# Scores over 128 rows for three of four batches, and value blocks 144 and 160 bytes apart, in a hashed attention with a gated feed-forward

## The chip, the core and the metric

The kernel runs on one core of a Trainium2 chip. The metric is the device time of one execution in microseconds (us); the median of three runs stands for a kernel. A core has TensorE (PE in the profile; its weight loads are PEld), VectorE (DVE), ScalarE (ACT), GpSimd (POOL) and SyncE (SP), and 16 DMA engines that all its queues share. SP issues most DMAs here, on queue q1; POOL issues the loads of the feed-forward weights, on queue q0.

## What is computed

```python
# q, k, v: (4, 8, 768, 64) f32; proj: (64, 6) f32
q_bits = (einsum('bhsd,dk->bhsk', q, proj) > 0)
k_bits = (einsum('bhsd,dk->bhsk', k, proj) > 0)
mask = q_bucket[:, :, :, None] == k_bucket[:, :, None, :]   # the six bits as one number
scores = where(mask, q @ k.T / 8, -1e9)
attn = exp(scores - max); attn = attn / (sum(attn) + 1e-9)
x = (attn @ v).transpose(0, 2, 1, 3).reshape(3072, 512)
xn = x / sqrt(mean(x * x) + 1e-6) * rms_g
out = (silu(xn @ w_gate) * (xn @ w_val)) @ w_out
```

## The kernel before

**Scores with the mask inside.** For each pair of heads a tile `QK` (fp16) holds, per head, 768 columns of q and 768 of k. Rows 0 to 63 are the head's dimensions and rows 64 to 69 six bits as plus or minus 16 (`KROWS` = 70). One product over 70 rows gives scores in which unequal bits are pushed far down, so that the exponential (`probs`, line 333) with a fixed bias needs no other mask. `scores` (line 317) makes two such products, of 128 keys by 384 queries each, into two PSUM banks.

**Values.** `av` (line 337) multiplies 128x128 blocks of probabilities, as weights, with blocks of 64 value columns and a column of ones (65 columns, fp16): 18 for each head and half batch, 1,152 in all. The blocks lie in `vls`, two tiles [128, 8 heads, 6, 66], one for even and one for odd batches: 66 columns of two bytes, 132 bytes from block to block.

**The feed-forward.** For each half batch, `gate` and `value` make 128x384 blocks of the hidden layer, `project` the output, 512 columns wide, and `store` writes it out through SP.

**The order of work.** It is written out by hand. The program runs through 192 slots; in slot t TensorE gets the two score products of slot t+1, ScalarE the exponential of slot t, and then whatever stands in the plan for t. `at(0, t, f, ...)` puts a step into slot t, and `spread` shares the feed-forward's products out over the slots. Each engine works through its list in this order, without passing one instruction by another, so a step that waits holds up all that stands behind it on its engine.

**The inputs of a pair.** q and k of a pair are loaded by SP, two transfers (`kn`, `qn`) in batch 0 and the first half of batch 1, eight smaller ones (`qL`, `kL`) after that, and v in one (`vn`). They are turned by TensorE (`turn_pe`, line 137, for pairs (0,0) to (1,1)) or by VectorE (`turn_dve`), and cast into `QK` by POOL or VectorE. The bits come from a product with `proj` and a sign operation on VectorE into a tile `bits`, and SP moves them into rows 64 to 69 of `QK`: four transfers of six rows for a pair in `send` (line 261), eight in `hash_one` (line 281). (b, hp) means head pair hp of batch b.

**The buffers of QK.** Six come from a pool, `qkpool`, in turn: pair number 4b + hp uses buffer (4b + hp) mod 6. The loads of pair (1,1) stand in slot 20, those of (1,2) in 34, of (1,3) in 45 and of (2,0) in 50; the bits of (1,2) are made in slot 51, those of (1,3) in slot 61. The first scores of pair (1,2) are those of slot 60, of pair (1,3) those of slot 66.

SP lets at most eight of its DMAs be under way: each one waits for the one eight before it.

Of the kernel before, what the change touches and what calls it, by code (L numbers as in the profile page):

```python
# [9 lines left out]
FP16 = mybir.dt.float16  # L10
# [6 lines left out]
H = 8  # L17
S = 768
# [4 lines left out]
HALF = 384  # L23
# [10 lines left out]
def kernel(  # L34
# [12 lines left out]
    nc = tc.nc  # L47
    PSUM = bass.MemoryType.PSUM

    const = ctx.enter_context(tc.tile_pool(name="const", bufs=1))  # L50
    lpool = ctx.enter_context(tc.tile_pool(name="lpool", bufs=8))
    tpool = ctx.enter_context(tc.tile_pool(name="tpool", bufs=2))
    qkpool = ctx.enter_context(tc.tile_pool(name="qkpool", bufs=6))
    ppool = ctx.enter_context(tc.tile_pool(name="ppool", bufs=3))
    xpool = ctx.enter_context(tc.tile_pool(name="xpool", bufs=2))
    npool = ctx.enter_context(tc.tile_pool(name="npool", bufs=1))
# [11 lines left out]
    zeros16 = const.tile([128, 512], FP16, name="zeros16")  # L68
# [5 lines left out]
    wg = const.tile([128, 4, DFF], FP16, name="wg")  # L74
    wv = const.tile([128, 4, DFF], FP16, name="wv")
    wo = const.tile([128, NF, DMODEL], FP16, name="wo")
    vls = [const.tile([128, H, 6, 66], FP16, name=f"vl{i}") for i in range(2)]
    vsum = [const.tile([128, H, 66], FP16, name=f"vsum{i}") for i in range(2)]
    cvb = [const.tile([128, H, 66], FP32, name=f"cvb{i}") for i in range(2)]

    def bank(name, shape=None, dt=FP32):
# [43 lines left out]

    PARITY = (0, 1)
    ONPE = [(0, hp) for hp in range(4)] + [(1, 0), (1, 1)]
    KROWS = D + 6  # L130
    qT, kT, QK = {}, {}, {}

    def new_pair(b, hp):
        qT[b, hp] = tpool.tile([128, S], FP32, name="qT")
        kT[b, hp] = tpool.tile([128, S], FP32, name="kT")
        t = qkpool.tile([128, 2, 2 * S], FP16, name="QK")
        QK[b, hp] = t
        for hh in range(2):
            QK[b, 2 * hp + hh, "h"] = t[:, hh, :]

    def turn_pe(b, hp, hh, which, keep=nc.vector.tensor_copy, act=()):

        src = raw[b, hp][0 if which == "q" else 1][:, hh].rearrange(
            "p (j e) d -> p j (e d)", e=2
        )
        ps = bank("t_ps", [128, 3, 128])
        for j in range(3):
            nc.tensor.transpose(ps[:, j, :], src[:, j], ident)  # L148
        psf = ps.rearrange("p j t -> p (j t)")
        keep(turned(b, hp, which)[:, hh, :], psf)  # L150
        o = 0 if which == "q" else S
        for e in act:
            nc.scalar.copy(
                QK[b, 2 * hp + hh, "h"][0:64, o + e * HALF : o + (e + 1) * HALF],
                psf[64 * e : 64 * e + 64, :],
            )
# [12 lines left out]
    def turn_dve(b, hp, which, part, parts=4):  # L169

        src = raw[b, hp][0 if which == "q" else 1]
        dst = (qT if which == "q" else kT)[b, hp]
        if b in PARITY:
            nc.vector.transpose(
# [140 lines left out]
    def scores(u, i):  # L315
        b, half = divmod(u, 2)
        h, ch = divmod(i, 3)
        ps = scps.tile([128, 2, 512], FP32, name="s_ps")
        for j in range(2):
            jt = 2 * ch + j  # L320
            nc.tensor.matmul(  # L321
                ps[:, j, 0:HALF],
                QK[b, h, "h"][0:KROWS, S + jt * 128 : S + (jt + 1) * 128],
                QK[b, h, "h"][0:KROWS, half * HALF : (half + 1) * HALF],
                start=True, stop=True,
            )
        sps[u, i] = ps
# [10 lines left out]
    def av(u, h, part):  # L338
# [5 lines left out]
        for i in range(9 * part, 9 * part + 9):  # L344
# [3 lines left out]
                psb[u, h][:, jt, c * 128 : (c + 1) * 128],  # L348
                vls[b % 2][:, h, 2 * (jt % 3) + jt // 3 if b in PARITY else jt, 0:65],
                start=(hh == 0 and i == 0), stop=(jt == 5),  # L350
# [110 lines left out]
    def rows_of(u, c):  # L461
        b, half = divmod(u, 2)
        rows = out[b * S : (b + 1) * S, :].rearrange("(p c) n -> p c n", c=6)
        return rows[:, 2 * c + half if b in PARITY else 3 * half + c, :]

# [69 lines left out]
    def at(w, s, f, *a):  # L535
        plan[NS * w + s].append(lambda: f(*a))

    new_pair(0, 0)
    turn_pe(0, 0, 0, "k", act=(0,))
    turn_pe(0, 0, 0, "q", act=(0,))  # L540
# [8 lines left out]
    for which, e in (("k", 0), ("q", 0), ("k", 1)):  # L549
        direct(which, e)  # L550
    scores(0, 0)
    _, direct1, _, _ = hash_direct(0, 0, (1,))

# [29 lines left out]
    for hp, s0 in ((1, 2), (2, 8), (3, 13)):  # L583
        at(0, s0, new_pair, 0, hp)
        at(0, s0, turn_pe, 0, hp, 0, "k")
        at(0, s0 + 1, turn_pe, 0, hp, 1, "k")
        at(0, s0 + 1, cast_pool, 0, hp, "k")
        at(0, s0 + 2, turn_pe, 0, hp, 0, "q")
        at(0, s0 + 3, turn_pe, 0, hp, 1, "q")
        at(0, s0 + 3, cast_part, 0, hp, "q", 0, 0, 2, nc.vector)  # L590
        at(0, s0 + 3, cast_part, 0, hp, "q", 1)
        at(0, s0 + 4, hash_pair, 0, hp)
        if hp == 1:
            at(0, s0 + 5, send_pair, 0, hp, (1,))
            at(0, s0 + 5, move_head, 0, hp, 0)
        else:
            at(0, s0 + 5, send_pair, 0, hp)
# [16 lines left out]
    for hp, ts in ((0, (8, 22, 23, 24, 25, 24, 26, 26, 28, 42)), (1, (20, 27, 28, 29, 30, 29, 41, 32, 33, 43))):  # L614
        tl, ts = ts[0], ts[1:]
        for w in "kq":
            at(0, tl, load_natural, nc.sync, 1, hp, w)
        at(0, tl, load_v, nc.sync, 1, hp)
        at(0, ts[0], new_pair, 1, hp)
        for t, hh, w in zip(ts[0:4], (0, 1, 0, 1), "kkqq"):  # L620
            at(0, t, turn_pe, 1, hp, hh, w)
        at(0, ts[4], cast_pool, 1, hp, "k")
        at(0, ts[5], cast_pool, 1, hp, "q")
        if hp == 0:
            at(0, ts[6], hash_pair, 1, hp)
            at(0, ts[7], send_pair, 1, hp)
        at(0, ts[8], v_prep, 1, hp)
        at(0, ts[8], v_sum, 1, hp)
# [10 lines left out]
        (3, 2): (114, (135, 136, 137, 139), (140, 141, 142, 143), 145),  # L639
        (3, 3): (132, (144, 145, 147, 153), (153, 154, 154, 155), 156),  # L640
    }
    TX = 37
    sqs = {}

# [7 lines left out]
    for n, (u, h) in enumerate(order):  # L652
        t = 3 * n + 4 - ((u, h) == (0, H - 1))
        for part in range(2):
            at(0, t + part, av, u, h, part)
        if h % 2:
            if (u, h) == (0, H - 1):
# [6 lines left out]
                at(0, t + 2, norm, u)  # L664
                at(0, TX, norm_third, u, 2, nc.scalar.mul)
                at(0, TX + 1, send_pair, 1, 1)
                at(0, TX - 1, idle, 2, bank)
                at(0, TX, idle, 1, bank)
                for c in range(3):
                    at(0, TX, turn_x, u, c, c == 2)  # L670
                continue
# [13 lines left out]
    def spread(t0, n, pieces):  # L685
        fixed = [SCORES + (AV if (t - 1) % 3 < 2 else 0) for t in range(t0, t0 + n)]
        extra = [(t, *inserts.pop(t)) for t in range(t0, t0 + n) if t in inserts]
        total = sum(fixed) + sum(p[0] for p in pieces) + sum(e[1] for e in extra)
        i, done = 0, 0
        for s in range(n):  # L690
            done += fixed[s]
            while i < len(pieces):
                weight, whole, steps = pieces[i]
                full = done + weight // 2 > total * (s + 1) // n
                if extra and whole and t0 + s >= extra[0][0] and (full or extra[0][1] > MEAN):
                    _, weight, *step = extra.pop(0)
                    at(0, t0 + s, *step)
                    done += weight
                    continue
                if full:  # L700
                    break
                done += weight
                for delay, *step in steps:
                    at(0, t0 + s + delay, *step)
                i += 1
        for _, _, *step in extra:
            at(0, t0 + n - 1, *step)
        assert i == len(pieces)

    for u in range(7):  # L710
# [4 lines left out]
        if u == 0:  # L715
            t0 = TX + 1
            spread(t0, 2 * NS - t0, gates)
# [4 lines left out]
        for i in range(9):  # L722
            c, n = divmod(i, 3)
# [12 lines left out]
    def behind_norm(t):  # L736

        return t - t % NS + 7 if 1 <= t % NS < 7 else t

    for (b, hp), (load, kturns, qturns, _) in spots.items():  # L740
# [7 lines left out]
        t = behind_norm(qturns[-1] + 2)  # L748
# [10 lines left out]
    for t in range(LAST):  # L759
        if t + 1 < LAST:  # L760
            scores(*head_of(t + 1))
        probs(*head_of(t))
        for f in plan[t]:
            f()
# [50 lines left out]
```

## Time and profile before

| | us |
|---|---|
| three runs | 337.41, 338.36, 678.17 |
| median of the runs | 338.36 |
| profiled execution, its own time | 338.97 |
| its span, first to last instruction | 335.5 |
| PE busy | 327.7 |
| ACT busy | 224.6 |
| DVE busy | 239.7 |
| POOL busy | 149.6 |

The profile is of one execution. A group line has: line, engine, operation, tile written <- tiles read, partitions x elements and type, x count, then busy time, mean ns of one instruction, and the engine's idle time just before the group with what ended most of it. A timeline line has: start and duration in us, engine, line, operation, tiles, shapes and how many instructions were merged. SPq lines are DMAs that SP issues; their duration is that of the issue, not of the transfer. For TensorE, busy time is not the same as throughput: its products overlap, and what one costs is the time from its start to the start of the next.

### The profile page before, as it was taken

To read this page: it belongs to the slowest core of one execution; us is meant where nothing else is said; L and a number is where in the kernel's file an instruction comes from. 1 tells how busy PE (TensorE), PEld (TensorE's weight loads), DVE (VectorE), ACT (ScalarE), POOL (GpSimd) and SP (SyncE) were. 2 spreads that over 40 slices of the span, in tenths; PEclk is the share of its full clock that TensorE was granted. 3 is DMA by queue.
4 is the path that set the end of the run, shared out by engine and by line. 5 is a ranking of instruction groups with operands and counts; after the bars stand their busy time and mean duration, and the time that the engine had idled before them with its cause. 6 is when DMAs were issued, how large, how long until landed. Compare 5 with 4: busy or idle time off the path is not lost.

```text
span 335.5 us, 7802 instructions
## 1 busy us (share of the span) xinstructions
PE 327.7 (98%) x3004; PEld 197.9 (59%) x3004; DVE 239.7 (71%) x491; ACT 224.6 (67%) x326; POOL 149.6 (45%) x201
## 2 busy tenths in 40 slices
PE   7899999999999999999999999999999999999996
PEld 4566756655566565655656556655656566664554
DVE  2898786778878669866888568886776456674870
ACT  2887887676767666767667667776676867754322
POOL 3466949418733644736383622747471111122000
PEclk9999999999999999999999999999999999999999
DMA  7940999969308736151717027001100010002002
GB/s 247 319 143 11 226 179 212 210 120 185 115 17 150 127 108 129 31 118 65 129 53 141 6 96 142 7 2 38 63 4 3 3 63 33 0 2 76 21 0 94
DMA packets 79692, 30.92 MB, mean 92 GB/s; under 512 B 64988, under 2 KB 76712, under 8 KB 79656
## 3 DMA queue, kind: packets, MB, share of 16 engines
q1 hardware_dynamic: 75528, 25.45, 32.3%
q0 software_dynamic: 3680, 4.72, 8.3%
q8 instruction: 23, 0.38, 0.5%
q10 hardware_dynamic: 448, 0.27, 0.3%
q14 instruction: 13, 0.11, 0.1%
HBM read 28.32 MB, written 6.29 MB: 103 GB/s over the span
## 4 chain that ended last, share of the span: by engine, by line
PE 84%; DVE 6%; DMA 3%; SPq 2%; POOL 1%; ACT 1%; issue 1%; ACTq 0%; DVEq 0%; POOLq 0%
PE v_ps L427 18%; PE g_ps L427 17%; PE s_ps L321 16%; PE y_ps L456 16%; PE o_ps L346 9%; PE d_ps L202 2%; PE d_ps L222 2%; PE x_ps L410 2%; DMA QK<-bits 1%; SPq L281 1%; DVE xn L403 1%; PE t_ps L148 1%; DMA pj<-in_proj_dram 1%; ACT psb L333 1%; PE y_ps L475 1%
## 5 line engine op out<-in xcount | busy, mean ns | idle before, releaser
L333 ACT ACTIVATE psb<-s_ps,ebias 128x768 f16<-128x768 f32 x192 | 167.8, 899 | 23.9 <-PE s_ps L321 22.8
L321 PE MATMUL s_ps<-QK 70*128 70x384 f16 x384 | 93.6, 326 | 2.0 <-ACT psb L333 1.5
L435 ACT ACTIVATE t<-g_ps 128x384 f32<-128x384 f32 x96 | 47.1, 491 | 54.7 <-PE g_ps L427 54.5
L427 PE MATMUL g_ps<-xnT,wg 128*128 128x384 f16 x384 | 82.6, 325 | 0.1
L427 PE MATMUL v_ps<-xnT,wv 128*128 128x384 f16 x384 | 81.7, 325 | 0.2 <-DVE a L444 0.2
L444 DVE SCALAR_TENSOR_TENSOR a<-t,g_ps 128x384 f32<-128x384 f32 x96 | 52.7, 549 | 27.3 <-ACT t L435 25.7
L367 POOL TENSOR_TENSOR x<-otmp,rcp 128x384 f32<-128x384 f32 x31 | 25.9, 835 | 99.5 <-DVE rcp L365 99.0
L456 PE MATMUL y_ps<-wo,ht 128*128 128x512 f16 x276 | 68.0, 378 | 0.0
L346 PEld LDWEIGHTS <-psb 128*128 128x128 f16 x1152 | 52.1, 97 | 16.2 <-issue 1.4
L445 DVE SCALAR_TENSOR_TENSOR ht<-a,v_ps 128x384 f16<-128x384 f32 x96 | 53.2, 554 | 11.7 <-PE v_ps L427 3.5
L346 PE MATMUL o_ps<-vl,psb 128*128 128x65 f16 x1152 | 56.3, 193 | 0.0
L321 PEld LDWEIGHTS <-QK 70*128 70x128 f16 x384 | 34.6, 98 | 35.7 <-issue 12.0
L427 PEld LDWEIGHTS <-wv 128*128 128x128 f16 x384 | 35.2, 97 | 22.3 <-issue 1.4
L427 PEld LDWEIGHTS <-wg 128*128 128x128 f16 x384 | 34.7, 97 | 21.1 <-DVE xnT L416 0.6
L456 PEld LDWEIGHTS <-ht 128*128 128x128 f16 x276 | 24.7, 97 | 22.5
L372 POOL TENSOR_TENSOR sq<-x 128x384 f32<-128x384 f32 x31 | 25.8, 832 | 2.4
L468 ACT COPY ysb<-y_ps 128x512 f32<-128x512 f32 x23 | 13.5, 585 | 19.6 <-PE y_ps L456 19.6
L194 POOL CAST QK<-qT 64x768 f16<-64x768 f32 x20 | 16.6, 830 | 19.0 <-DVE qT L181 17.1
L360 DVE TENSOR_TENSOR otmp<-o_ps,cvb 128x390 f32<-128x390 f32 x32 | 17.8, 558 | 9.1 <-PE o_ps L346 8.8
L376 DVE TENSOR_REDUCE ssp<-sq 128x3 f32<-128x384 f32 x32 | 16.9, 529 | 9.8 <-POOL sq L372 9.6
L194 POOL CAST QK<-kT 64x768 f16<-64x768 f32 x20 | 16.5, 824 | 12.7 <-PE s_ps L321 7.3
L403 DVE TENSOR_SCALAR xn<-x,rstd 128x512 f16<-128x512 f32 x23 | 16.1, 754 | 6.8 <-POOL rstd L392 6.8
(72 smaller groups left out, 264.1 us busy)
## 6 DMA issues: line engine op xcount, KB each, us to landing
vn<-in_v_dram SPq DMA_DIRECT2D x16, 384.0 KB
out_dram<-ysb SPq DMA_DIRECT2D x23, 256.0 KB
qL<-in_q_dram SPq DMA_DIRECT2D x40, 96.0 KB
kL<-in_k_dram SPq DMA_DIRECT2D x40, 96.0 KB
kn<-in_k_dram SPq DMA_DIRECT2D x5, 384.0 KB
qn<-in_q_dram SPq DMA_DIRECT2D x5, 384.0 KB
wg<-in_moe_w_gate_dram POOLq DMA_DIRECT2D x2, 768.0 KB, 8.2
wv<-in_moe_w_val_dram POOLq DMA_DIRECT2D x2, 768.0 KB, 10.4
```

The costliest lines, as they stand in the source:

```text
L194: nc.gpsimd.tensor_copy(QK[b, 2 * hp + hh, "h"][0:64, o : o + S], src[64 * hh : 64 * hh + 64, :])
L321: nc.tensor.matmul(ps[:, j, 0:HALF], QK[b, h, "h"][0:KROWS, S + jt * 128 : S + (jt + 1) * 128], QK[b, h, "h"][0:KROWS, half * HALF : (half ...
L333: nc.scalar.activation(psb[u, h][:, 2 * ch : 2 * ch + 2, :], sps.pop((u, i))[:, :, 0:HALF], AF.Exp, bias=ebias, scale=ESCALE,)
L346: nc.tensor.matmul(o[:, c, hh, 0:65], psb[u, h][:, jt, c * 128 : (c + 1) * 128], vls[b % 2][:, h, 2 * (jt % 3) + jt // 3 if b in PARITY el ...
L367: eng.tensor_mul(xd.rearrange("p c (h d) -> p c h d", h=2), tmp[:, :, :, 0:64], r.to_broadcast([128, 3, 2, 64]),)
L372: eng.tensor_mul(sq, xd, xd)
L403: mul(xn[u][:, c, :], x[u][:, c, :], rstds[u][:, c : c + 1])
L427: nc.tensor.matmul(ps, w[:, kt, fs], xnT[u][:, kt, :], start=(kt == 0), stop=(kt == 3))
L435: nc.scalar.activation(t, fbank[u, ft, "g_ps"], AF.Tanh, scale=0.5)
L444: nc.vector.scalar_tensor_tensor(out=a, in0=t, scalar=1.0, in1=g, op0=ALU.add, op1=ALU.mult)
L445: nc.vector.scalar_tensor_tensor(out=ht[u][:, ft, :], in0=a, scalar=0.5, in1=vv, op0=ALU.mult, op1=ALU.mult)
L456: nc.tensor.matmul(y, ht[u][:, ft, c * 128 : (c + 1) * 128], wo[:, ft, :], start=(ft == 0), stop=(ft == NF - 1),)
```

## The change

The score products of batches 1 to 3 run over all 128 rows of `QK` instead of the first 70. Rows 70 to 127 of each buffer are filled with zeros once, by a new function `zero_rows`, which SP issues as one DMA from a tile of zeros: buffers 4 and 5 in slot 19, and buffers 0, 1, 2 and 3 in slots 49, 51, 56 and 60. So that the zeros stay, the six buffers become fixed tiles `qks` instead of a pool's. Scores of batch 0 stay at 70 rows. In `vls` the blocks become 72 (even batches) and 80 columns (odd batches) wide, of which 66 were allotted before and 65 are read: 144 and 160 bytes from block to block.

```diff
-    qkpool = ctx.enter_context(tc.tile_pool(name="qkpool", bufs=6))
...
-    vls = [const.tile([128, H, 6, 66], FP16, name=f"vl{i}") for i in range(2)]
+    vls = [const.tile([128, H, 6, n], FP16, name=f"vl{n}") for n in (72, 80)]
...
+    qks = [const.tile([128, 2, 2 * S], FP16, name=f"QK{i}") for i in range(6)]
...
-        t = qkpool.tile([128, 2, 2 * S], FP16, name="QK")
+        t = qks[(4 * b + hp) % 6]
...
+    def zero_rows(i):
+        nc.sync.dma_start(
+            out=qks[i][KROWS:128].rearrange("p h (n c) -> p (h n) c", c=512),
+            in_=zeros16[KROWS:128].unsqueeze(1).to_broadcast([128 - KROWS, 6, 512]),
+        )
...
+        rows = slice(0, 128 if b else KROWS)
         for j in range(2):
             jt = 2 * ch + j
             nc.tensor.matmul(
                 ps[:, j, 0:HALF],
-                QK[b, h, "h"][0:KROWS, S + jt * 128 : S + (jt + 1) * 128],
-                QK[b, h, "h"][0:KROWS, half * HALF : (half + 1) * HALF],
+                QK[b, h, "h"][rows, S + jt * 128 : S + (jt + 1) * 128],
+                QK[b, h, "h"][rows, half * HALF : (half + 1) * HALF],
                 start=True, stop=True,
             )
...
+    for i, t in ((4, 19), (5, 19), (0, 49), (1, 51), (2, 56), (3, 60)):
+        at(0, t, zero_rows, i)
```

In the program that results, the orders of TensorE, VectorE, ScalarE and POOL are those of before, and SP has six more DMAs. Those of buffers 4 and 5 follow the bits of pair (0,3) and stand ahead of `kn`, `qn` and `vn` of pair (1,1). Buffer 0's stands after `vn` of (1,3) and ahead of the first store and the loads of (2,0); buffer 1's between `vn` of (2,0) and the bits of (1,2); buffers 2's and 3's after those bits, with a store before each, and ahead of the bits of (1,3). The first score products that read a buffer over 128 rows wait for its zeros too.

## The prediction

> **What bounds the kernel now.** I read the busy times of the page first, then its chain of work, then TensorE's and SP's timelines around the edits, and last the DMA shares by window.
>
> ```profile
> PE 327.7 (98%) x3004; PEld 197.9 (59%) x3004; DVE 239.7 (71%) x491; ACT 224.6 (67%) x326; POOL 149.6 (45%) x201
> PE 84%; DVE 6%; DMA 3%; SPq 2%; POOL 1%; ACT 1%; issue 1%; ACTq 0%; DVEq 0%; POOLq 0%
> L321 PE MATMUL s_ps<-QK 70*128 70x384 f16 x384 | 93.6, 326 | 2.0 <-ACT psb L333 1.5
> L346 PE MATMUL o_ps<-vl,psb 128*128 128x65 f16 x1152 | 56.3, 193 | 0.0
> q1 hardware_dynamic: 75528, 25.45, 32.3%
> ```
>
> TensorE is busy 98% of the span and is 84% of the chain, and its two edited groups hardly wait (2.0 and 0.0 us). So whatever shortens a matmul's slot shortens the kernel, and whatever makes TensorE wait lengthens it: it issues in order and has nothing to catch up with. The timeline shows the slots:
>
> ```profile
> 202.01 0.49 PE L321 MATMUL s_ps<-QK 70*128 70x384 f16 x2
> 202.34 0.45 PE L346 MATMUL o_ps<-vl,psb 128*128 128x65 f16 x9
> 202.63 0.49 PE L427 MATMUL v_ps<-xnT,wv 128*128 128x384 f16 x2
> ```
>
> From start to start a pair of scores takes 0.33 us and nine value products 0.29: some 165 and 32 ns each, far under the 326 and 193 ns of single instructions, which overlap.
>
> **The value blocks.** Over 1,144 value products (start to start, gaps over 60 ns left out) the mean is 31.1 ns; the 285 whose block lies at a multiple of 16 bytes take 29.5. With 132 bytes between blocks one in four does; with 144 and 160 all do. 1,152 x 1.63 ns = 1.9 us, all on the path. The bounds are 0 (two aligned blocks never follow each other in this trace) and 1.9; I take 1.9.
>
> **The scores.** In batches 1 to 3, 144 pairs change from 70 to 128 rows. In the trace the first matmul of such a pair holds its slot for 166 or 167 ns in nearly all cases (from 161 to 174), the second for 162, as a 128-row gate product does. The excess over 162 ns adds up to 0.7 us for the 144 pairs, which I take as the gain, with 0 as the other bound. [...]
>
> **The zero transfers.** This is what I expect to decide. Six transfers are new on SP's queue, each 58 partitions x 6 x 1,024 bytes = 356 KB, from SBUF to SBUF. On how many of the 16 DMA engines does one run? The trace shows how rows are shared out. The q1 line counts 75,528 packets. The data of its transfers come to 72,780 (61,440 of 128 bytes for qL and kL, 7,148 of 1,536, 2,944 of 2,048, 480 of 768, 256 of the last stores, 512 of gcol). The other 2,748 are 4-byte end marks, one for each engine of a transfer: 135 transfers of 32 or 128 rows x 16 + 98 transfers of six bit rows x 6. So every transfer here is cut into equal shares: 16 where 16 divides the rows, 6 of 6. The numbers up to 16 that cut 58 = 2 x 29 rows equally are 1 and 2. I take 2 engines with 29 rows each; if shares may be unequal, it is 16. The trace has no such row count.
>
> [...]
>
> The rate:
>
> ```profile
> core 0: us, PE busy (x) PEld busy (x) DVE busy (x) ACT busy (x) POOL busy (x), PEclk, DMA share, GB/s
> 35.50:38.50 3.00, 3.00 (x47) 1.87 (x46) 2.43 (x6) 2.37 (x4) 2.78 (x5) 1.00 1.03 349
> 39.00:42.00 3.00, 3.00 (x53) 2.63 (x51) 2.20 (x5) 2.96 (x5) 2.78 (x4) 1.00 1.16 209
> ```
>
> 349 GB/s with 16 engines full is 21.8 per engine, 47 ns for 1,024 bytes (the last stores' 1,024-byte packets take 47 too). On two engines a zero transfer takes 356 / 43.6 = 8.2 us; on 16 it takes 1.0. Every load that SP issues afterwards has a sixteenth of its bytes on those same two engines, behind the zeros, and lands only then.
>
> **First place: buffers 4 and 5.** In the new order of SP they stand behind the eight bit transfers and ahead of the loads of pair (1,1):
>
> ```profile
> 24.29 8.76 SPq L261 DMA_DIRECT2D QK<-bits  x8
> 33.10 0.45 SPq L94 DMA_DIRECT2D kn<-in_k_dram  x1
> 33.65 0.40 SPq L94 DMA_DIRECT2D qn<-in_q_dram  x1
> 34.09 0.47 SPq L103 DMA_DIRECT2D vn<-in_v_dram  x1
> 38.53 2.83 SPq L261 DMA_DIRECT2D QK<-bits  x4
> ```
> ```profile
> 37.66 0.49 PE L321 MATMUL s_ps<-QK 70*128 70x384 f16 x2
> 37.99 0.49 PE L148 MATMUL t_ps<-ident,kn 128*128 128x128 f32 x3
> ```
>
> The transpose of kn at 37.99 is in TensorE's order, so nothing behind it can run. By the trace's packet records kn's data now begin at 34.2 and its 256 packets are through by about 36.4: 1.6 us to spare. Afterwards the two engines hold zeros from 34.4, for 16.4 us; and the first halves of wg and wv, moving from 38.4 to 46.5 in the trace, want the same engines for 8.6 us (64 packets each at 134 ns). From 57 to 64, where a queue of loads and one of weights are full together, both advance one packet for one. So the zeros end at 34.4 + 16.4 + 8.6 = 59.4, kn's share takes 1.1 more, and TensorE waits from 37.99 to 60.5: 22.5 us. The bits of (1,0) land meanwhile and cost nothing more. The lower bound is 13.5 (the zeros go first: they end at 50.8 instead).
>
> **Second place: buffers 0 to 3.** Times here are those of before, to which the first wait is added. The wait leaves SP time to work off its queue, so buffer 0's zeros run ahead of (2,0)'s loads and I cost them nothing. Buffer 1's stand between vn of (2,0) (82.47) and the bits of (1,2):
>
> ```profile
> 82.47 0.58 SPq L103 DMA_DIRECT2D vn<-in_v_dram  x1
> 83.16 5.78 SPq L281 DMA_DIRECT2D QK<-bits  x8
> 89.04 0.85 SPq L469 DMA_DIRECT2D out_dram<-ysb  x2
> 92.86 5.66 SPq L281 DMA_DIRECT2D QK<-bits  x8
> ```
>
> The first four land at about 86.9 and are read by the scores at 87.13: 0.2 us of cover. The two engines finish the loads at 84, then hold zeros until 92.2; a six-row transfer has one row on each, if it uses the same engines. The scores wait until 92.3, or 95 if SP is itself held while the queue is full (issues of 4.3 to 4.8 us at 49 to 62 us show such holds): 5.2 to 7.9, I take 6.5. Buffers 2 and 3 follow, with a store between: 95 to 111.5. The bits of (1,3) stand behind them and land at 111.5 to 114; their scores, at 96.72 before, would come at 103.2 and wait 8.3 to 11; I take 9.5. Together 16, with 24 as the upper bound if SP gains no lead. Zeros also precede scores by their own semaphores, but the bits behind them are later.
>
> **The clock.** The first eight idle products of 512 columns (1.18 to 4.56 us) start 427 ns apart, later ones 216: half the clock after idling. After three waits over 6 us the same could cost 0 to 2.4 us each (up to 4.8 us at half pace); I take 4 in all.
>
> **The rest.** Fixed buffers in place of the pool: engine orders other than SP's are the same, and Pool's casts lose waits for DMAs and keep those for TensorE, 0.
>
> **Sum.** The profiled execution took 338.97 us (span 335.5): - 1.9 - 0.7 + 22.5 + 16 + 4 = 378.9. It stands 0.6 above the median of 338.36, so I predict 378.3.
>
> **The rivals.**
>
> 1. The zeros keep the weights out of the two engines. In the trace wg's data began at 38.4, as q1's loads ended, which speaks for it; the one-for-one stretch speaks against. The first wait is 13.5, and the time 369.
> 2. SP gains no lead, and buffer 0's zeros delay the loads too: 24 and 3 for held issues in the second place instead of 16: 389; packets at 60 ns instead of 47 would lead to about 400.
> 3. The other side: each zero transfer is spread unevenly over 16 engines. Nothing in the trace forbids it; no transfer there does it. Then 1.0 us each: kn lands 2 us later (two issues of 0.66, two transfers partly beside them) against 1.6 to spare, 0.5 lost; the bits of (1,2) land 1.3 to 2.1 later against 0.2, 1.6 lost; the gap of SP from 89.9 to 92.86 hides the rest. 338.4 - 2.6 + 2.1 = 337.9. It decides from about 13 engines on, where two zeros cost no more than the 2.6 us gained.
> 4. As 3, with the zeros wholly hidden: 335.8.
>
> **How the numbers follow.** The forecast has 0.55, rival 1 0.20, rival 2 0.11, rivals 3 and 4 0.14. The range 355 to 400 holds the first three, but for the odd 0.05 of them. A measurement of this kernel can tell about 2% (6.8 us) from no change. Slower 0.86, same 0.13, faster 0.01.
>
> **What would show it.** Right: TensorE idle for over 10 us before the transpose of kn near 38 us, released by a DMA; two more waits at scores whose bits land late; DMA share near 2/16 in those stretches; value products at 29.5 ns and pairs of scores at 324 in batches 1 to 3. Wrong: no long idle on TensorE, and zero transfers with 16 end marks, or loads that pass the zeros.

## The result, and the profile after

| | us |
|---|---|
| before, runs beside after (a further one of 678.17 is left out of the comparison) | 337.41 to 338.36 |
| after, four runs: lowest, median, highest | 385.44, 386.68, 388.6 |
| ratio of after to before | 1.146, 95% interval 1.141 to 1.150 |
| after, profiled execution: own time, span | 387.02, 385.2 |

The change costs 49 us. The forecast was 378.3 with a range from 355 to 400.

The page of after, the lines that answer to those of before (busy times, the granted clock in 40 slices, the chain, the two edited groups, SP's queue):

```profile
PE 332.5 (86%) x3004; PEld 200.4 (52%) x3004; DVE 240.3 (62%) x491; ACT 225.0 (58%) x326; POOL 149.9 (39%) x201
PEclk9999555999996877999999999999999999999999
q1 hardware_dynamic: 77628, 27.59, 29.7%
PE 71%; DMA 14%; DVE 6%; SPq 4%; POOL 2%; issue 1%; ACT 1%; DVEq 0%; ACTq 0%; POOLq 0%
L329 PE MATMUL s_ps<-QK 128*128 128x384 f16 (+1 forms) x384 | 95.2, 331 | 21.9 <-DMA QK<-bits 19.9
L354 PE MATMUL o_ps<-vl,psb 128*128 128x65 f16 x1152 | 56.8, 195 | 0.0
```

TensorE's busy time hardly moved (327.7 to 332.5), but it is 86% of the span and no longer 98%: it stands still for 45 us more. In the chain DMAs went from 3 to 14%. The clock line has two dips at half rate or between, where TensorE has been idle.

What TensorE waited for in after:

```profile
PE t_ps L155 <- DMA kn<-in_k_dram: 24.9, 1, 24.9
PE s_ps L329 <- DMA QK<-bits: 19.9, 2, 11.1
```

And its timeline at these three places (start, duration, and in brackets the idle time before and what ended it):

```profile
37.55 0.49 PE L329 MATMUL s_ps<-QK 70*128 70x384 f16 x2
62.99 0.88 PE L155 MATMUL t_ps<-ident,kn 128*128 128x128 f32 x3 [24.95 <-DMA kn<-in_k_dram]
...
67.19 0.49 PE L329 MATMUL s_ps<-QK 70*128 70x384 f16 x2
...
125.35 0.80 PE L329 MATMUL s_ps<-QK 128*128 128x384 f16 x2 [11.08 <-DMA QK<-bits]
...
145.31 0.80 PE L329 MATMUL s_ps<-QK 128*128 128x384 f16 x2 [8.78 <-DMA QK<-bits]
```

Three waits, all ended by DMAs, at the transposes of `kn` and at the scores that need the bits of (1,2) and of (1,3). Behind each wait TensorE runs at half clock for a while: the pair of scores at 125.35 lasts 0.80 us instead of 0.49.

The simplest way to see where the time went is to set the start of each of the 192 pairs of scores beside its start in before. The difference stays constant wherever nothing is lost:

```
pair of scores      28     29     31     48     60     61     66     68    191
before, start    37.66  38.32  40.23  66.95  87.13  88.70  96.72 100.03
after - before   -0.11  25.34  26.97  26.97  38.22  39.66  48.59  50.40  49.61
```

First place: 25.4 us, and 1.6 of half clock behind it. Second place: 11.3 and 8.9, with 1.4 and 1.8 of half clock. From pair 68 to pair 191 after gains 0.8. The sum, -0.1 + 25.4 + 1.6 + 11.3 + 1.4 + 8.9 + 1.8 - 0.8 = 49.5, is the difference of the spans (49.7) but for 0.2. The profiled times differ by 48.05, as 3.5 us of before's lay outside its span and 1.8 of after's.

SP's timeline around the first place:

```profile
24.19 8.77 SPq L268 DMA_DIRECT2D QK<-bits  x8
33.00 5.18 SPq L143 DMA_DIRECT2D QK<-zeros  x2
38.22 15.95 SPq L94 DMA_DIRECT2D kn<-in_k_dram  x1
54.28 0.61 SPq L94 DMA_DIRECT2D qn<-in_q_dram  x1
54.94 0.67 SPq L103 DMA_DIRECT2D vn<-in_v_dram  x1
```

The second zero transfer holds SP for 4.4 us, and the issue of `kn` takes 15.95 us where it took 0.45. Behind the zeros SP itself stands still.

How many DMA engines carried the zeros is read in the q1 line, as the forecast read it: 77,628 packets are the 75,528 of before, 6 x 348 rows of zeros, and 12 more. Twelve end marks for six transfers are two engines each. The windows of the stretches in which mainly zeros moved (PEclk, the share of the 16 engines in use, and GB/s stand last):

```profile
core 0: us, PE busy (x) PEld busy (x) DVE busy (x) ACT busy (x) POOL busy (x), PEclk, DMA share, GB/s
40.00:47.00 7.00, 0.00 (x0) 0.00 (x0) 0.00 (x0) 0.00 (x0) 1.54 (x2) 0.50 0.77 144
47.00:55.00 8.00, 0.00 (x0) 0.00 (x0) 0.00 (x0) 0.00 (x0) 0.00 (x0) 0.50 0.19 41
115.00:124.00 9.00, 0.00 (x0) 0.00 (x0) 1.16 (x2) 0.00 (x0) 4.33 (x6) 0.69 0.14 38
```

From 47 to 55 and from 115 to 124 TensorE does nothing, about two sixteenths of the DMA engines are in use, and they move some 40 GB/s. From 40 to 47 the weights fill the other engines, and they have a share of these two as well: by the packet records 11 to 14 rows of zeros move in each us from 40 to 50, and 42 to 48 in each from 51 to 55, when the weights are through. By the packet records the zeros of buffers 4 and 5 move from 34.4 to 61.3, those of buffer 0 from 97.6 to 107.4, those of buffer 1 from 114.3 to 124.3, and those of buffers 2 and 3 from 127.5 to 144.3.

### The profile page after: what moved, and what is told of

Read it like the earlier page. It is cut to its first block, busy times and chain, and to the rows that moved or that the text cites. A ratio compares the mean times of both kernels' runs of the same rounds, so it can differ in the third digit from the quotient of the medians.

```text
span 385.2 us, 7837 instructions
## 1 busy us (share of the span) xinstructions
PE 332.5 (86%) x3004; PEld 200.4 (52%) x3004; DVE 240.3 (62%) x491; ACT 225.0 (58%) x326; POOL 149.9 (39%) x201
## 3 DMA queue, kind: packets, MB, share of 16 engines
q1 hardware_dynamic: 77628, 27.59, 29.7%
## 4 chain that ended last, share of the span: by engine, by line
PE 71%; DMA 14%; DVE 6%; SPq 4%; POOL 2%; issue 1%; ACT 1%; DVEq 0%; ACTq 0%; POOLq 0%
PE g_ps L435 15%; PE v_ps L435 15%; PE s_ps L329 14%; PE y_ps L464 13%; PE o_ps L354 8%; DMA kn<-in_k_dram 6%; DMA QK<-zeros 4%; DMA QK<-bits 2%; PE d_ps L209 2%; PE d_ps L229 1%; DMA kL<-in_k_dram 1%; SPq L143 1%; PE t_ps L155 1%; SPq L117 1%; PE x_ps L418 1%
## 5 line engine op out<-in xcount | busy, mean ns | idle before, releaser
L329 PE MATMUL s_ps<-QK 128*128 128x384 f16 (+1 forms) x384 | 95.2, 331 | 21.9 <-DMA QK<-bits 19.9
L435 PE MATMUL g_ps<-xnT,wg 128*128 128x384 f16 x384 | 83.7, 329 | 0.1
L435 PE MATMUL v_ps<-xnT,wv 128*128 128x384 f16 x384 | 82.8, 329 | 0.2 <-DVE a L452 0.2
L329 PEld LDWEIGHTS <-QK 128*128 128x128 f16 (+1 forms) x384 | 34.8, 99 | 56.2 <-issue 33.2
L354 PEld LDWEIGHTS <-psb 128*128 128x128 f16 x1152 | 53.0, 99 | 16.3 <-issue 2.1
L155 PE MATMUL t_ps<-ident,kn 128*128 128x128 f32 x36 | 7.0, 310 | 24.9 <-DMA kn<-in_k_dram 24.9
L157 DVE COPY kT<-t_ps 128x384 f32<-128x384 f32 x12 | 6.5, 551 | 30.5 <-PE t_ps L155 30.5
L476 ACT COPY ysb<-y_ps 128x512 f32<-128x512 f32 x23 | 13.5, 586 | 19.4 <-PE y_ps L464 19.4
```

The source lines that it names most:

```text
L329: nc.tensor.matmul(ps[:, j, 0:HALF], QK[b, h, "h"][rows, S + jt * 128 : S + (jt + 1) * 128], QK[b, h, "h"][rows, half * HALF : (half + 1) ...
L354: nc.tensor.matmul(o[:, c, hh, 0:65], psb[u, h][:, jt, c * 128 : (c + 1) * 128], vls[b % 2][:, h, 2 * (jt % 3) + jt // 3 if b in PARITY el ...
L435: nc.tensor.matmul(ps, w[:, kt, fs], xnT[u][:, kt, :], start=(kt == 0), stop=(kt == 3))
```

## The experiments

Times are set against runs of before on the same chip; each number in a row of waits is total, count and longest. The theory: the zero transfers lose the time, because 58 rows are cut for two DMA engines and the loads and bits behind them in SP's queue wait for these two. Rivals: the wider scores (by power and clock), the copy's bytes and not its engines, the later waits as an echo of the first, and a loss that the two busy engines cause on whichever queue.

**1. The zero transfers alone**

```diff
-    vls = [const.tile([128, H, 6, n], FP16, name=f"vl{n}") for n in (72, 80)]
+    vls = [const.tile([128, H, 6, 66], FP16, name=f"vl{i}") for i in range(2)]
...
-        rows = slice(0, 128 if b else KROWS)
+        rows = slice(0, KROWS)
```

> The changed kernel, but with all scores over 70 rows and value blocks 132 bytes apart: what is left of the change is the fixed buffers and the six zero transfers (nothing reads the zeros). Theory (the zero transfers alone cost the time): the same waits as in the changed kernel, 25 us ahead of the transposes of kn and some 11 and 9 us at the scores of the bits of (1,2) and (1,3), granted clock about 0.94, and 386.7 + 0.7 + 0.8 = about 388 us. Rival (scores over 128 rows draw more power, the granted clock falls to 0.94 by that, or the new blocks collide with something): no long wait, clock near 1.0 and about 338 us.

Measured: 387.0 us, ratio 1.145 (1.141 to 1.149), clock 0.94. What TensorE waited for:

```profile
PE t_ps L155 <- DMA kn<-in_k_dram: 24.9, 1, 24.9
PE s_ps L329 <- DMA QK<-bits: 15.7, 2, 8.0
```

Nothing reads these zeros, and the time is that of the whole change. The wider scores and the blocks have no part in the loss: without them the granted clock is 0.94 as it is with them. The size of the later waits is not the same in every run: 8.0 and 7.7 us here, 11.1 and 8.8 in the trace of the whole change. A row of the zeros of buffers 0 and 1 took 50 ns on the mean here and 60 there.

**2. 56 rows instead of 58**

```diff
-            out=qks[i][KROWS:128].rearrange("p h (n c) -> p (h n) c", c=512),
-            in_=zeros16[KROWS:128].unsqueeze(1).to_broadcast([128 - KROWS, 6, 512]),
+            out=qks[i][KROWS:126].rearrange("p h (n c) -> p (h n) c", c=512),
+            in_=zeros16[KROWS:126].unsqueeze(1).to_broadcast([126 - KROWS, 6, 512]),
...
-        rows = slice(0, 128 if b else KROWS)
+        rows = slice(0, 126 if b else KROWS)
```

> The changed kernel, but the zeros fill rows 70 to 125 (56 rows instead of 58) and the scores of batches 1 to 3 run over 126 rows: 3% fewer bytes. Theory (58 = 2 x 29 rows are cut for two DMA engines, 56 = 14 x 4 for 14): the end marks on the queue show 14 per zero transfer instead of 2, each zero transfer takes 344 KB / (14 x 21.8 GB/s) = 1.1 us instead of 8 to 10, the long waits go, and the time is 336 to 339 us, about that of the kernel before. Rival (a copy within SBUF is slow by its bytes or its direction, or SP is held by issuing it): nearly the same waits, 385 us.

Measured: 349.26 us, ratio 1.033 (1.030 to 1.036). TensorE's first wait and the queue:

```profile
PE t_ps L155 <- DMA kn<-in_k_dram: 9.2, 1, 9.2
```
```profile
q1 hardware_dynamic: 77628, 27.52, 33.3%
```

The packets are 75,528 + 6 x 336 rows + 84 end marks (that the total is that of after is chance: 12 rows fewer and 12 end marks more for each transfer), so 14 engines for each, as expected, and two rows fewer take 37 us off. But the time is 10 to 13 us above the expected one. The later waits are gone; ahead of `kn` 9.2 us are left, which experiments 7 and 8 take up.

**3. 57 rows**

The same edit with 127 for 126.

> The changed kernel, but the zeros fill rows 70 to 126 (57 rows) and the scores of batches 1 to 3 run over 127 rows. Theory (57 = 3 x 19 rows are cut for three engines): 3 end marks per zero transfer, 5.4 us each with the engines alone; ahead of the transposes of kn two of them, 10.7 us, and 5.7 us of the weights on the same three engines: a wait of about 18 us, then some 6 and 4 us at the later scores and 3 to 4 us of half clock; 366 to 372 us. Rival (the count of engines does not matter, bytes do): 386 us. Rival (uneven shares are possible for 57 rows, so 15 or 16 engines): 337 us.

Measured: 368.18 us, ratio 1.090 (1.086 to 1.093).

```profile
PE t_ps L155 <- DMA kn<-in_k_dram: 18.8, 1, 18.8
PE s_ps L329 <- DMA QK<-bits: 8.2, 2, 5.1
```
```profile
q1 hardware_dynamic: 77598, 27.55, 30.9%
```

The packets are 75,528 + 6 x 342 rows + 18 end marks, so three engines for each transfer. The first wait is as worked out (about 18 us); the later ones are 3.0 and 5.1 us where some 6 and 4 were. From 58 to 57 to 56 rows the bytes fall by 3% and the time goes from 386.7 to 368.2 to 349.3: it goes by the divisor of the row count, which is 2, 3 and 14.

**4. The zeros on another queue**

```diff
-        nc.sync.dma_start(
+        nc.scalar.dma_start(
```

> The changed kernel, but the six zero transfers are issued by ScalarE on its own queue; still 58 rows, on two engines. Theory (the loads and bits are late because they stand behind the zeros in the same queue's order on those two engines; on another queue they share the engine packet by packet): the waits fall to a few us, 340 to 350 us, and two engines stay full of zeros for as long as before. Rival (what counts is that two engines are busy, whoever's queue it is): the same waits, about 385 us.

Measured: 377.32 us, ratio 1.117 (1.113 to 1.120): by the time, much nearer to the rival.

```profile
PE o_ps L354 <- DVE otmp L368: 10.6, 1, 10.6
PE s_ps L329 <- DMA vn<-in_v_dram: 8.1, 1, 8.1
PE s_ps L329 <- ACT psb L341: 6.2, 5, 4.1
```
```profile
47.08 2.83 SPq L268 DMA_DIRECT2D QK<-bits  x4
50.01 24.96 SPq L117 DMA_DIRECT2D qL<-in_q_dram  x4
75.01 5.08 SPq L117 DMA_DIRECT2D kL<-in_k_dram  x4
```
What SP waited for, and ScalarE's timeline near 35 us:
```profile
SPq L117 <- DMA QK<-zeros: 20.5, 1, 20.5
SPq L268 <- DMA QK<-zeros: 10.2, 1, 10.2
```
```profile
30.08 4.75 ACTq L143 DMA_DIRECT2D QK<-zeros  x2
34.89 2.69 ACT L341 ACTIVATE psb<-s_ps,ebias 128x768 f16<-128x768 f32 x3 [3.91 <-issue]
```

The long wait for `kn` is gone: `kn` lands at 43.8 us and not at 62.9, though the zeros of the first place move until 70.8. So for the first place the order in the queue is what counts, as the theory says. Other losses come in its stead. ScalarE, which issues the zeros now, is held by that itself, and TensorE waits 4.1 us for its exponential near 35. The rule that at most eight DMAs are under way counts those of both queues here: the bits of (1,0) and the second `qL` are issued only when the first and the second zero transfer have landed (47.0 and 71.2). So 20.5 of the 24.96 us of the four `qL` issues lie between the first and the second, in which SP issues nothing; in before the four took 6.2. And where the two queues do share engines, they share them packet for packet: from 55.5 to 57 us the packet records show 57 rows of zeros and 58 packets of `qL`, and a packet of `qL` has 128 bytes where one of zeros has 1,024. From 86 to 116 us zeros and the loads of (1,3) and (2,0) are under way together, and a `kL` transfer issued at 97.05 lands 12.5 us later. The theory's price of 340 to 350 us is refuted, but this run does not weigh the shared engines against the waits that the new place of the zeros brings with it.

**5. Two engines in the first place alone**

```diff
+        if i < 4:
+            for r0, r1 in ((KROWS, 126), (126, 128)):
+                nc.sync.dma_start(
+                    out=qks[i][r0:r1].rearrange("p h (n c) -> p (h n) c", c=512),
+                    in_=zeros16[r0:r1].unsqueeze(1).to_broadcast([r1 - r0, 6, 512]),
+                )
+            return
```

> The changed kernel, but buffers 0 to 3 get their zeros as 56 rows (14 engines) and 2 rows (two engines, six packets each); buffers 4 and 5 keep 58 rows on two engines. Theory (each place costs for itself, and the run over 126 rows showed no wait in the second place): the wait ahead of the transposes of kn stays 25 us with some 1.6 us of half clock behind it, the two waits at the scores of (1,2) and (1,3) go, and the time is 338 + 25.3 + 1.6 - 1.4 = 363.5 us. Rival (the later waits are an echo of the first, because the first one shifts SP's order of work): 375 us or more.

Measured: 365.06 us, ratio 1.081 (1.078 to 1.083).

```profile
PE t_ps L162 <- DMA kn<-in_k_dram: 24.6, 1, 24.6
```

The half clock behind this wait costs 2.0 us, and no pair of scores later loses more than 0.1. The two places cost each for itself: 27 us the first, and 22 the second, by which the whole change is slower still.

**6. The blocks alone**

```diff
-    vls = [const.tile([128, H, 6, 66], FP16, name=f"vl{i}") for i in range(2)]
+    vls = [const.tile([128, H, 6, n], FP16, name=f"vl{n}") for n in (72, 80)]
```

(on the kernel before)

> The kernel before, with value blocks 144 and 160 bytes apart and nothing else of the change. Prediction's step: 1.9 us less (336.1, value products at 29.5 ns each). Theory from the trace after: products of batches 2 and 3 go from 31.7 to 30.5 ns, those of batches 0 and 1 stay at 30.4, about 0.8 us less (337.2).

Measured: 336.88 against 337.63 us, ratio 0.997 (0.996 to 0.998), that is 0.7 to 1.4 us less. In the trace, from pair 60 on, the gaps from one value product to the next fall from 31.3 to 30.4 ns on the mean, 0.7 us in all for 729 of them. The gain is real, and less than the forecast's 1.9.

**7. Zeros earlier**

The 126 rows of experiment 2, and:

```diff
-    for i, t in ((4, 19), (5, 19), (0, 49), (1, 51), (2, 56), (3, 60)):
+    for i, t in ((4, 14), (5, 14), (0, 14), (1, 14), (2, 22), (3, 22)):
```

> The run over 126 rows (14 engines), but with all six zero transfers issued earlier: four behind the bits of (0,2), two behind vn of (1,1), where the kernel before has few bytes on its way. Theory (a zero transfer costs only what the loads behind it lose; in that run the loads of pair (1,1) lost the 3 us ahead of the weights and then shared the engines with them one for one): no wait over 2 us on TensorE, and 338 - 1.4 = 336.6 us, at most 339. Rival (copies within SBUF cost something wherever they stand, through SP's held issues or the bits behind them): 342 us or more.

Measured: 347.37 us, ratio 1.028 (1.025 to 1.030): the rival.

```profile
PE s_ps L329 <- DMA QK<-bits: 7.1, 1, 7.1
```
```profile
core 0: us, PE busy (x) PEld busy (x) DVE busy (x) ACT busy (x) POOL busy (x), PEclk, DMA share, GB/s
29.00:36.00 7.00, 4.18 (x62) 2.99 (x55) 3.75 (x9) 4.06 (x5) 5.04 (x6) 1.00 0.86 168
```

It shows what was missing. For 7 us hardly anything but zeros moves, on 14 engines, and they move 168 GB/s, half of the 349 that the loads get in before. So a transfer of 344 KB takes some 2.05 us and not 1.1, four of them 8.2 us. TensorE waits 7.1 us for the bits of (0,3) behind them, and the half clock after that wait costs 3.1 more. No run here moved the zeros to other rows or took them from another place, so the halving is measured and its cause is not.

**8. The weights later**

The 126 rows of experiment 2, and:

```diff
-    for i, t in enumerate((22, 34)):
+    for i, t in enumerate((27, 34)):
```

> The run over 126 rows, but the first halves of wg and wv are issued by GpSimd five slots later, behind the work of pair (1,0). There zeros moved at about 166 GB/s from 35.9 to 40 us, the weights' data came from 37.5 on, and the loads of pair (1,1) then shared the engines with them one packet for one: 9.2 us of wait ahead of the transposes of kn. Theory (the weights' share is most of that wait): kn's 393 KB follow the zeros at full rate and land near 42 us, a wait of 2 to 4 us; the first gate and value products wait some us for their weights instead. Rival (the copying itself or SP's held issues are the wait): still 8 to 9 us.

Measured: 344.63 us, ratio 1.020 (1.016 to 1.025).

```profile
PE t_ps L155 <- DMA kn<-in_k_dram: 4.4, 1, 4.4
```
```profile
core 0: us, PE busy (x) PEld busy (x) DVE busy (x) ACT busy (x) POOL busy (x), PEclk, DMA share, GB/s
34.50:37.00 2.50, 2.50 (x39) 1.65 (x35) 1.94 (x4) 2.50 (x4) 1.87 (x3) 1.00 0.80 184
40.00:42.00 2.00, 0.00 (x0) 0.00 (x0) 0.00 (x0) 0.00 (x0) 1.85 (x3) 0.50 1.00 352
```

With the weights out of the way the loads of pair (1,1) run at 352 GB/s behind the zeros, and the wait falls from 9.2 to 4.4. So the 9.2 us of experiment 2 are about half the slow copy and half a lost place: the loads, 4 us late, no longer pass before the weights, and share the engines with them.

**9. Zeros by instructions**

```diff
     def zero_rows(i, eng=nc.gpsimd):
-        nc.sync.dma_start(
...
+        eng.memset(qks[i][64:128], 0.0)
...
+    for i in range(2):
+        zero_rows(i, nc.vector)
...
-    for i, t in ((4, 19), (5, 19), (0, 49), (1, 51), (2, 56), (3, 60)):
+    for i, t in ((2, 1), (3, 1), (4, 5), (5, 5)):
```

> The changed kernel without zero transfers: rows 64 to 127 of the six buffers are set to zero once by instructions, two buffers by VectorE at the start (idle there from 1.6 to 5.5 us), four by GpSimd in its first gaps; scores of batches 1 to 3 over 128 rows, blocks as changed. Theory (the rest of the change gains, only the transfers cost): 0.65 us less by the scores and 0.8 us less by the blocks, 336.6 us, no long wait, clock as before. Prediction's own terms: 2.6 us less, 335.4. Rival (128 rows draw so much that the clock falls, or the fixed buffers cost): 338 us or more.

Measured: 339.96 us, ratio 1.007 (1.005 to 1.008). No long wait and a clock of 1.00, so nothing of the 49 us is left; but 3.0 us are lost by pair 40 and only 0.8 gained from there. GpSimd's memsets run at 16 bits an element:

```profile
11.57 5.25 POOL L143 MEMSET QK<- 64x3072 f16 x2
...
19.73 5.78 POOL L143 MEMSET QK<- 64x3072 f16 x2
```

**10 and 11. The same with 32-bit zeros, with and without the blocks**

```diff
-        eng.memset(qks[i][64:128], 0.0)
+        eng.memset(qks[i][64:128].bitcast(FP32), 0.0)
```

> As the run with memsets, but the four memsets of GpSimd write 32-bit zeros (1,536 elements a row instead of 3,072 of 16 bits). In that run each pair of them held GpSimd for 5.3 and 5.8 us and put TensorE 2.4 us behind by the scores of slot 18, while from slot 48 on it gained 0.8 us. Theory (GpSimd's time goes by elements, so a pair takes 2.7 to 2.9 us and fits its idle 3 us; rows and blocks gain): no delay in batch 0, 337.6 - 1.4 = 336.2 us, at most 337.0. Rival (128 rows and blocks gain nothing, or the memsets delay batch 0 all the same): 337.6 us or more.

> The kernel with 32-bit memsets and value blocks 132 bytes apart: of the change, scores of batches 1 to 3 over 128 rows and the fixed buffers alone. Prediction's step and the trace after: the first matmul of a pair at 162 instead of 167 ns, 0.65 us less, 337.0 us. Rival (a weight load goes by columns, rows gain nothing): 337.6 us.

Measured: 339.29 us, ratio 1.006 (1.004 to 1.008), with the blocks; 339.34, ratio 1.006 (1.004 to 1.008), without. Both rivals by their times. But the traces tell two things apart. From pair 60 on the run without blocks has first matmuls of a pair at 163.2 instead of 166.9 ns on the mean and second ones at 162.4 instead of 161.7, 0.4 us less in all. In experiment 1, with the same fixed buffers and 70 rows, the first take 166.9. So rows do count in the slot, by 3 ns for a pair. In the weight load they do not: in the trace of before one of 128 columns of 16 bits takes 98 ns with 70 rows and 97 with 128, while with 128 rows of 32 bits one takes 108 ns with 32 columns and 148 to 151 with 128. And the loss lies in one spot of batch 0. Of the run with blocks, VectorE's and GpSimd's timelines there:

```profile
17.99 2.45 DVE L256 COPY QK<-bits 6x768 f16<-6x768 f16 x2
```
```profile
17.32 2.91 POOL L143 MEMSET QK<- 64x1536 f32 x2
```

**12. The last two memsets elsewhere**

```diff
-    for i, t in ((2, 1), (3, 1), (4, 5), (5, 5)):
+    for i, t in ((2, 1), (3, 1), (4, 12), (5, 17)):
```

> As the run with 32-bit memsets, but GpSimd's last two stand later, in its gaps near 25 and 31.5 us. In that run VectorE's two copies of bits near 18 us took 2.45 instead of 0.72 us while the memsets ran on GpSimd from 17.3 to 20.2, and TensorE waited 1.8 us behind them; from there on the kernel gained 0.8 us. Theory (that overlap is what was lost): no wait for otmp, the copies of bits at 0.72 us again, 337.5 - 0.8 to 1.4 = about 336.5 us. Rival (rows and blocks gain less than the memsets cost wherever they stand): 337.5 us or more.

Measured: 337.57 against 337.51 us, ratio 0.999 (0.998 to 1.000).

```profile
18.43 0.72 DVE L256 COPY QK<-bits 6x768 f16<-6x768 f16 x2
```

The two copies are back at 0.72 us and TensorE's wait of 1.8 us behind them is gone: the overlap with the memsets was the loss. The gain of 0.8 us from pair 48 on is there, but 0.6 us were lost ahead of it, of which 0.4 at the norm near pair 39. At best the wider scores with the blocks, brought in without any transfer, cannot be told from no change. Of all versions that ran, only the blocks alone (experiment 6) beat the kernel before, by 0.3%.

## Why the prediction was right, and where it was off

1. *Two engines for 58 rows.* Right: 12 end marks for six transfers, and 57 and 56 rows give 3 and 14 (experiments 2 and 3).
2. *First place, 22.5 us.* Measured 25.4. The zeros began at 34.4 as forecast, and the two engines were shared with the weights, but they ended at 61.3 and not at 59.4: a row of zeros took 60 ns on the mean and not 47, and 85 to 87 from 56 to 60 us, while `kn`, `qn` and `vn` were loading. Rival 1, zeros that keep the weights out, is refuted by the 11 to 14 rows a us beside the weights. (By the forecast's own terms its wait would have been 13.9 us and not 13.5: 50.8 + 1.1 - 38.0.)
3. *Second place, 6.5 and 9.5 us.* Measured 11.3 and 8.9. The step that failed is "buffer 0's zeros run ahead of (2,0)'s loads and I cost them nothing". They moved from 97.6 to 107.4 and held SP at the first loads of (2,0) for 6.98 us instead of 3.75. So `vn` of (2,0) was issued 2.9 us ahead of the scores that wait for the bits behind it, where before had 4.7; buffer 1's zeros began at 114.3, just when these scores were due, and took 9.9 us instead of 8.2. This part of rival 2 (SP gains no lead) came true, at 5 us instead of its 11. Its size varies: in experiment 1, where the rows of these zeros took 50 ns, `vn` was issued 3.9 us ahead and the first wait was 8.0 us. What made a row take 60 ns here is not known; from 115 to 119 us no other packet was on the three queues that the program uses.
4. *Half clock, 4 us.* Measured 1.6 + 1.4 + 1.8 = 4.8.
5. *Scores, -0.7.* From pair 60 on, the first product of a pair takes 3.7 ns less and the second 0.7 more, 0.4 us for 132 pairs (experiments 10 and 11). The other bound, 0, does not hold for the slot, though the weight load itself takes 98 ns with 70 rows and 97 with 128 in before.
6. *Value blocks, -1.9.* Mis-sized: 29.5 ns for an aligned block came from blocks whose neighbours were not aligned. With all aligned, three products in four take 29 or 30 ns, but in batches 2 and 3 one in five takes 35, most of them at the same four places of the eighteen, and the mean stays at 30.5. In batches 0 and 1, which were at 30.5 already, nothing is gained; in 2 and 3 some 1.25 ns each, 0.7 us.
7. *Rival 3, 16 engines and 337.9 us.* It did not come about, and its price was wrong too: 14 engines cost 349.3. It took 349 GB/s for zeros that move at 168 to 184, and left the weights out, which share the engines with the loads when these are late (experiment 2: 9.2 us of wait ahead of `kn`; 4.4 with the weights later, experiment 8).

The sum: first place +2.9 against the forecast, second +4.2, clock +0.8, gains short by 1.7, less 1.6 for what lies outside the span, make 8 of the 8.1 us between 378.9 and 387.02. The waits came out longer but for one (8.9 for 9.5). Each was priced by rows of 47 ns; those of buffers 4, 5, 0 and 1 took 60 on the mean and those of buffers 2 and 3, behind which the 8.9 us were lost, 49.

## What to carry to other kernels

Before adding a DMA, look at how its row count divides: of rows that have no divisor near 16, leave some out or cut the transfer in two, and check it by the count of end marks (here 58 rows ran on 2 engines, 57 on 3 and 56 on 14, in 386.7, 368.2 and 349.3 us). A transfer in front of loads costs what those loads lose, including their place ahead of the next large transfer, so look at what starts soon after them. And a pattern that is good for single instructions (an aligned block among unaligned ones) is to be tried on all of them before its gain is counted.

## What the runs showed of the hardware that was not expected

- One DMA's issue held SP for 15.95 us (`kn`, behind two zero transfers on two engines); without zeros it took 0.45.
- Zeros from SBUF to SBUF over 14 engines move at 168 to 184 GB/s (experiments 7 and 8), loads from DRAM at 349 to 352. On 14 engines a row of zeros takes 83 ns on the mean in experiment 7; on two it takes 47 from 51 to 55 us of after, 22 GB/s for each engine, so this slower pace showed with 14 engines and not with two.
- VectorE's two copies of bits took 2.45 us beside GpSimd's memsets (experiment 10) and 0.72 away from them (experiment 12). In experiment 10 they end at 18.9 and 20.4 us, each 0.2 us behind the end of a memset.
- GpSimd's memset took half the time with half the elements: 64 rows x 6,144 bytes took 2.6 to 2.9 us at 16 bits an element, 1.35 to 1.46 at 32 (means of a pair, experiments 9 and 10).
